# One wide score product per chunk and head for items 0 to 7 of a linear-attention kernel, and end tables turned ahead of item 0's own products

## The chip, the cores and the metric

The kernel runs on one NeuronCore of a Trainium2 chip. The metric is the device time of one execution in microseconds (us), measured from outside the program; a profile's span (first to last instruction) is a little shorter. All data is float32.

## The reference

Two layers follow each other. The first is a linear attention with a decaying state (B = 4 batches, H = 8 heads, S = 768 tokens, head size 48):

```python
for t in range(S):
    kt, vt, rt = (k[:, :, t], v[:, :, t], r[:, :, t])
    cur = np.einsum('bhd,bhe->bhde', u[None] * kt, vt)
    y[:, :, t] = np.einsum('bhd,bhde->bhe', rt, state + cur)
    state = w[None, :, :, None] * state + np.einsum('bhd,bhe->bhde', kt, vt)
```

The second sends each token (the 384 values of its 8 heads) to one of 8 experts, `max(x @ w1[e], 0) @ w2[e]`, scaled by a softmax gate; a sigmoid decides whether a token takes its own best expert or that of its predecessor. The change touches the first layer alone.

## The kernel before, in words

**Work items.** The attention is cut into 16 items: one batch and one pair of heads each (`n = b * HP + hp`, HP = 4). The two heads of a pair lie on partitions 0 to 47 and 64 to 111. The 768 tokens are 6 chunks of 128. For one item, TensorE (PE) does these stages:

- `scores` (L284 to 299): for each chunk the products of all its keys with all its queries, into one of two PSUM pairs of banks, three chunks each (`g` = 0 and 1). VectorE (DVE) multiplies each group by a mask, `kept`, into the SBUF tile `am` (L299), so that only earlier keys count.
- `own` (L267): the product of each token with its own key, times `vT` on DVE (L282), into the output bank `y`.
- `added` (L250): what each chunk adds to the state, into PSUM `T`, and `states` (L260): the running state over chunks, a scan on DVE.
- `inside` (L301): `am` times the values, added to `y`. `before` (L310): the state ahead of each chunk times the decayed queries `rw`, added to `y`. ScalarE (ACT) then copies `y` to `xT` (L327).
- `turn` (L332): transposes of the output, two ACT copies, and for the last pair of a batch a DMA to DRAM. `logits` (L345): the router's products, once per batch.

**Around them.** GpSimd (POOL) makes three tiles per item in `scale` (L205): `rw` (queries times powers of the decay), `ke` (keys times powers of the decay, from the table `endT`), `pd` (queries times keys). DVE makes `kw`, the keys divided by the powers (L246); for items 0 to 2 it makes `rw` too. `endT` holds each head's end powers with tokens on partitions: `ends` copies them out of the power table on ACT (L168, L169), `turn_ends` (L171) transposes them on PE and copies the result on ACT (L176).

**The order.** `run` (L362) writes the order of every engine's instructions out by hand, so each engine's queue holds what the code says in that order. In the step of item n the code issues, among others, `inside(n-1)`, `before(n-1)`, `scores(n+1)` (from n = 5 on; `scores(n)` before that), `own(n)`. In the step of item 0 it is `scores(0)`, `own(0)`, `turn_ends` for the three other head pairs, `warm(3)` (three transposes of the identity), `added(0)`. `banks` (L186) hands out the two PSUM pairs in turn, one per call. Loads of an item (`rk`, `kv`, `vT`) are issued on SyncE's queue three items ahead. After item 15 the experts follow, in one stream without a barrier.

**The score products of before.** A chunk's 128 keys are taken as two halves of 64 (L291 to 298). The first half meets all 128 queries, the second only the last 64, since earlier queries do not see later keys (item 0 takes all 128 for both). Each product is 48 rows by 64 columns of PE's array, and so uses one quarter of it: the row half follows from the head, the column half from `f = c % 2 ^ o`. In odd chunks the two halves change places, so that the long product falls on either column half in turn; the host stores the tokens of `k` and `v` of odd chunks with their halves swapped (`_tokens`, L1764), and `kept` has a second mask for them (L1693 to 1696). There are 24 such products per item. A float32 product is two matmul instructions in the trace, each with its weight load.

The parts that the change touches:

Of the kernel before, what the change touches and what calls it, by code (L numbers as in the profile page):

```python
# [20 lines left out]
P = 128  # L21
B, H, S, DH = 4, 8, 768, 48
HP = H // 2
DP = 64
# [25 lines left out]
W_LO, W_HI = 0.8, 1.25  # L50
C2 = NCH // 2
AHEAD = 4
VB = NCH * 2 * DH
LATE = (B * HP - 2, B * HP - 1)

# [7 lines left out]
class Attention:  # L63
# [127 lines left out]
    def load(self, n):  # L191
        nc = self.nc
        b, hp = divmod(n, HP)
        rk, vT, kv = self.rks[n % AHEAD], self.vTs[n % AHEAD], self.kvs[n % (AHEAD + 1)]
        if n:
            nc.sync.dma_start(out=rk.rearrange("p a c t -> p (a c t)"), in_=self.rk_d[b, hp])
        else:
            for z in (slice(0, C2), slice(C2, NCH)):
                nc.sync.dma_start(out=rk[:, :, z], in_=self.rk_d[b, hp].rearrange("p (a c t) -> p a c t", a=2, c=NCH)[:, :, z])
        nc.sync.dma_start(out=kv, in_=self.kv_d[b, hp])  # L200
        nc.sync.dma_start(out=vT.rearrange("p a c t -> p (a c t)"), in_=self.vT_d[b, hp])
        self.items[n].update(b=b, hp=hp, rT=rk[:, 0], kT=rk[:, 1], vT=vT,
                             k=kv[:, :VB].rearrange("p (c x) -> p c x", c=NCH), v=kv[:, VB:])

    def scale(self, n, ahead=None):  # L205

        nc, t = self.nc, self.items[n]
        t["ke"] = self.two.tile([P, NCH, 2 * DH], F32, name="ke")
        t["pd"] = self.two.tile([P, NCH, P], F32, name="pd")
        t["rw"] = self.four.tile([P, NCH, P], F32, name="rw")  # L210
        hp = t["hp"]

        def ke(p):
            z = slice(p, NCH if n == 0 else NCH - 1, 2)
            nc.gpsimd.tensor_mul(t["ke"][:, z], t["k"][:, z], spread(self.endT[:, p, hp], 1, len(range(NCH)[z])))  # L215

        def pd(i):
            z = slice(i * C2, (i + 1) * C2)
            nc.gpsimd.tensor_mul(t["pd"][:, z], t["rT"][:, z], t["kT"][:, z])  # L219
# [64 lines left out]
    def scores(self, n, g):  # L284

        nc, t = self.nc, self.items[n]
        if g == 0:
            t["am"] = self.two.tile([P, 2, 2, 3, P], F32, name="am")
        sc = self.banks("sc")[:, :, :3 * P].rearrange("p h (c t) -> p h c t", t=P)
        for i in range(3):  # L290
            c = 3 * g + i  # L291
            for o in range(2):
                for h in range(2):
                    q, f = slice(h * DP, h * DP + DH), c % 2 ^ o

                    x = o * DP if n else 0
                    nc.tensor.matmul(sc[f * DP:(f + 1) * DP, h, i, x:], lhsT=t["kw"][q, c, o * DP:(o + 1) * DP],  # L297
                                     rhs=t["rw"][q, c, x:], start=True, stop=True)
        return lambda: nc.vector.tensor_mul(t["am"][:, g], sc, spread(self.kept[:, g:g + 3], 1, 2))  # L299

    def inside(self, n):  # L301
        nc, t = self.nc, self.items[n]
# [59 lines left out]
    def run(self, router, fetch, heads):  # L362
# [162 lines left out]
def general_attention(tc, rk_d, kv_d, wu, wg_d, x_d, ident, lt):  # L525

    nc = tc.nc
    with tc.tile_pool(name="g1", bufs=1) as g1, tc.tile_pool(name="g2", bufs=2) as g2, \
         tc.tile_pool(name="gy", bufs=1, space=PSUM) as gy, \
         tc.tile_pool(name="gps", bufs=2, space=PSUM) as gps:  # L530
        ones = g1.tile([P, 2], F32, name="g_ones")
        nc.vector.memset(ones, 0.0)
        for i in range(2):
            nc.vector.memset(ones[i * DP:(i + 1) * DP, i:i + 1], 1.0)
        turned = g1.tile([P, P], F32, name="g_turned")
        nc.vector.tensor_copy(turned[:, :DP], ident[:, DP:])
        nc.vector.tensor_copy(turned[:, DP:], ident[:, :DP])
        with tc.For_i(0, HP, 1) as hp:
            wu_t = g1.tile([P, 2], F32, name="g_wu")
            nc.sync.dma_start(out=wu_t, in_=wu[bass.ds(hp, 1)].rearrange("o p x -> (o p) x"))  # L540
            with tc.For_i(0, B, 1) as b:
                def of(ap):
                    return ap[bass.ds(b, 1), bass.ds(hp, 1)].rearrange("o q p x -> (o q p) x")

                r_t = g1.tile([P, S], F32, name="g_r")
                k_t = g1.tile([P, S], F32, name="g_k")
                v_t = g1.tile([P, NCH, 2, DH], F32, name="g_v")
                nc.sync.dma_start(out=r_t, in_=of(rk_d)[:, :S])
                nc.sync.dma_start(out=k_t, in_=of(rk_d)[:, S:])
                nc.sync.dma_start(out=v_t.rearrange("p c i e -> p (c i e)"),  # L550
                                  in_=of(kv_d)[:, 2 * NCH * DH:4 * NCH * DH])
                yp = gy.tile([P, 2, 512], F32, name="g_y")
                for e in range(DH):
                    vp = gps.tile([P, 2, 512], F32, name="g_vp")
                    for c in range(NCH):
                        for i in range(2):
                            nc.tensor.matmul(
                                vp[i * DP:(i + 1) * DP, c // 3, (c % 3) * P:(c % 3 + 1) * P],
                                lhsT=v_t[:, c, i, e:e + 1].to_broadcast([P, DP]),
                                rhs=turned if c % 2 else ident,  # L560
                                start=True, stop=True)
                    kv = g2.tile([P, S], F32, name="g_kv")
                    nc.vector.tensor_mul(kv.rearrange("p (g t) -> p g t", g=2),
                                         k_t.rearrange("p (g t) -> p g t", g=2), vp[:, :, :3 * P])
                    sv = g2.tile([P, S + 1], F32, name="g_sv")
                    nc.vector.memset(sv[:, 0:1], 0.0)
                    nc.vector.tensor_tensor_scan(sv[:, 1:], wu_t[:, 0:1].to_broadcast([P, S]), kv, 0.0,
                                                 Alu.mult, Alu.add)
                    z = g2.tile([P, S], F32, name="g_z")
                    nc.vector.scalar_tensor_tensor(z, kv, wu_t[:, 1:2], sv[:, :S], Alu.mult, Alu.add)  # L570
                    nc.vector.tensor_mul(z, z, r_t)
                    for c in range(NCH):
                        o = (c % 3) * 2 * DH + 2 * e
                        nc.tensor.matmul(yp[:, c // 3, o:o + 2], lhsT=z[:, c * P:(c + 1) * P], rhs=ones,
                                         start=True, stop=True)
                y = g1.tile([P, 2, 3, 2, DH], F32, name="g_ys")
                for g in range(2):
                    for i in range(2):
                        nc.vector.tensor_copy(
                            y[:, g, :, i, :],  # L580
                            yp[:, g, :6 * DH].rearrange("p (c e i) -> p c e i", c=3, i=2)[:, :, :, i])
                nc.sync.dma_start(
                    out=x_d.rearrange("(b c p) (h j) -> b h p c j", b=B, p=P, h=HP)
                    [bass.ds(b, 1), bass.ds(hp, 1)].rearrange("o q p c j -> (o q p) c j"),
                    in_=y.rearrange("p g c i e -> p (g c) (i e)"))
# [1178 lines left out]
def _tokens(a, np):  # L1764

    x = a.reshape(B, HP, 2, NCH, 2, DP, DH)
    x = np.stack([x[:, :, :, c, ::-1 if c % 2 else 1] for c in range(NCH)], 2)
    return x.transpose(0, 1, 4, 5, 2, 3, 6).reshape(B, HP, P, NCH * 2 * DH)


# [35 lines left out]
```

## Time and profile before

| | |
|---|---|
| time, three runs | 376.53, 377.59, 377.77 us (median 377.59) |
| the profiled execution | 378.4 us, of which the span is 376.7 us |
| TensorE clock granted, mean | 0.996 of full speed |
| PE busy | 361.5 us, 96% of the span |
| DVE, ACT, POOL busy | 244.8, 110.5, 152.3 us |
| attention | to about 107 us of the span, then the experts |

In the views below, a row of the timeline gives the start in us, the busy time in us, the engine, the line of the kernel, the operation, the tiles written and read, the shapes, and behind x the number of instructions merged in the row; in brackets stands how long the engine was idle before it and what ended the wait. PE is the matmul, PEld the weight load that belongs to it; "issue" means that the profile shows nothing that the engine waited for. The busy time of a row of matmuls includes the flight of the last one (some 0.2 to 0.3 us), so the length of a stage is read from its start to the start of the next.

### The profile page before, as it was taken

Reading aid. Unit: us, or ns where it says so; the run is one execution under the profiler, and the core shown is the slowest. Engines: PE = TensorE matmul, PEld = TensorE weight load, DVE = VectorE, ACT = ScalarE, POOL = GpSimd, SP = SyncE. Lnnn points to the kernel's source line nnn. Section 1 sums busy time; section 2 is a strip of 40 time slices with the busy share of each in tenths; the row PEclk is TensorE's granted clock in tenths of the full one; section 3 lists DMA queues with packets and bytes.
Section 4 is the critical chain, followed back from the end, with each engine's and each line's share of the span. In section 5 each row is a group of like instructions: output and inputs, shape, how many; then the busy total and the mean of one; then the engine's idle time right before and its main releaser. Section 6 shows DMA issues by size and latency. Waiting matters only on the chain. (4 is left out here: it accounts for less than half of the span.)

```text
span 376.7 us, 9667 instructions
## 1 busy us (share of the span) xinstructions
PE 361.5 (96%) x3844; PEld 318.7 (85%) x3844; DVE 244.8 (65%) x711; ACT 110.5 (29%) x304; POOL 152.3 (40%) x212
## 2 busy tenths in 40 slices
PE   7998899999999999999999999999999999999992
PEld 6766777777769998989899999999999998989971
DVE  6887778788834835886557666857767767555300
ACT  4222232223523212322332233333243233331210
POOL 8789999789512055212333113313233023021012
PEclk9999999999999999999999999999999999999998
DMA  7999998992568748713352452264165065072011
GB/s 256 411 407 408 404 409 314 338 357 106 196 194 298 269 169 336 260 35 127 121 198 62 155 216 78 56 218 186 36 209 220 14 220 202 19 259 114 2 41 37
DMA packets 17764, 74.93 MB, mean 199 GB/s; under 512 B 2778, under 2 KB 6624, under 8 KB 15408
## 3 DMA queue, kind: packets, MB, share of 16 engines
q1 hardware_dynamic: 10336, 56.89, 40.7%
q0 software_dynamic: 3424, 9.48, 7.3%
q10 hardware_dynamic: 3952, 7.87, 5.6%
q8 instruction: 32, 0.52, 0.6%
q14 instruction: 20, 0.16, 0.1%
HBM read 64.79 MB, written 9.47 MB: 197 GB/s over the span
## 5 line engine op out<-in xcount | busy, mean ns | idle before, releaser
L1358 POOL DMA_INDIRECT out_dram<-yo,sid x27 | 26.6, 985 | 115.8 <-ACT yo L1353 92.3
L1209 PE MATMUL h<-exT,w1t 128*128 128x168 f32 (+4 forms) x240 | 54.9, 327 | 0.0
L1213 DVE TENSOR_TENSOR hT<-h,hs 128x168 f32<-128x168 f32 (+3 forms) x60 | 21.1, 351 | 46.2 <-PE h L1209 29.6
L1132 POOL DMA_INDIRECT xg<-x_d,gid x29 | 31.2, 1076 | 30.3 <-DVE gid L899 19.2
L1209 PEld LDWEIGHTS h<-exT,w1t 128*128 128x128 f32 x240 | 41.6, 190 | 0.3 <-issue 0.3
L1159 PE MATMUL h<-exT,w1t 128*128 128x168 f32 (+2 forms) x192 | 37.3, 332 | 0.0
L299 DVE TENSOR_TENSOR am<-pair,kept 128x768 f32<-128x768 f32 x32 | 30.1, 953 | 11.0 <-PE pair L297 10.8
L1278 PE MATMUL y<-factors,sums 128*128 128x192 f32 x168 | 36.8, 326 | 0.0
L219 POOL TENSOR_TENSOR pd<-rk 128x384 f32<-128x384 f32 x32 | 31.8, 1014 | 8.9 <-PE y L276 6.3
L1209 PE MATMUL h<-xs,ws 128*128 128x168 f32 (+4 forms) x144 | 35.3, 327 | 0.0
L1159 PEld LDWEIGHTS h<-exT,w1t 128*128 128x128 f32 x192 | 30.9, 190 | 2.0 <-issue 0.2
L1278 PEld LDWEIGHTS y<-factors,sums 128*128 128x128 f32 x168 | 29.0, 190 | 0.2
L1209 PEld LDWEIGHTS h<-xs,ws 128*128 128x128 f32 x144 | 25.5, 190 | 4.3 <-ACT hs L1216 1.2
L297 PE MATMUL pair<-rw,kw 48*64 48x128 f32 (+1 forms) x768 | 23.4, 249 | 1.9 <-issue 1.7
L236 POOL TENSOR_TENSOR rw<-rk,tab 128x384 f32<-128x384 f32 x26 | 23.6, 930 | 0.4 <-DMA rk<-in_rk_dram 0.4
L306 PE MATMUL y<-am,kv 128*64 128x128 f32 x360 | 22.9, 276 | 0.3
L1278 PE MATMUL y<-w2t,hT 128*128 128x192 f32 x96 | 23.0, 328 | 0.0
L297 PEld LDWEIGHTS pair<-rw,kw 48*64 48x64 f32 x768 | 19.9, 133 | 3.4 <-issue 2.4
L1146 DVE COPY exT<-tp 128x384 f32<-128x384 f32 (+5 forms) x29 | 13.8, 485 | 13.2 <-PE tp L1145 13.1
L215 POOL TENSOR_TENSOR ke<-kv,endT 128x288 f32<-128x288 f32 (+1 forms) x32 | 21.8, 704 | 0.9 <-DMA kv<-in_kv_dram 0.9
L306 PEld LDWEIGHTS y<-am,kv 128*64 128x64 f32 x360 | 19.4, 137 | 2.2 <-issue 1.1
L327 ACT COPY xT<-y 128x768 f32<-128x768 f32 x15 | 12.0, 801 | 29.0 <-PE y L319 29.0
(304 smaller groups left out, 735.4 us busy)
## 6 DMA issues: line engine op xcount, KB each, us to landing
w1t<-in_w_dram SPq DMA_DIRECT2D x8, 1536.0 KB, 6.9
w2t<-in_w_dram SPq DMA_DIRECT2D x8, 1536.0 KB, 7.4
rk<-in_rk_dram SPq DMA_DIRECT2D x15, 768.0 KB, 10.3
kv<-in_kv_dram SPq DMA_DIRECT2D x16, 584.0 KB, 8.5
vT<-in_vT_dram SPq DMA_DIRECT2D x16, 384.0 KB, 6.3
x_d<-x ACTq DMA_DIRECT2D x4, 1152.0 KB
w1t<-in_w_dram SPq DMA_DIRECT2D x2, 768.0 KB
w2t<-in_w_dram SPq DMA_DIRECT2D x2, 768.0 KB, 5.2
```

Source lines behind the costliest of these rows:

```text
L215: nc.gpsimd.tensor_mul(t["ke"][:, z], t["k"][:, z], spread(self.endT[:, p, hp], 1, len(range(NCH)[z])))
L219: nc.gpsimd.tensor_mul(t["pd"][:, z], t["rT"][:, z], t["kT"][:, z])
L236: engine.tensor_mul(t["rw"][:, z], t["rT"][:, z], spread(pw, 1, z.stop - z.start))
L297: nc.tensor.matmul(sc[f * DP:(f + 1) * DP, h, i, x:], lhsT=t["kw"][q, c, o * DP:(o + 1) * DP], rhs=t["rw"][q, c, x:], start=True, stop=True)
L299: return lambda: nc.vector.tensor_mul(t["am"][:, g], sc, spread(self.kept[:, g:g + 3], 1, 2))
L306: nc.tensor.matmul(t["y"][h][p * DP:(p + 1) * DP, c2 * P:(c2 + 1) * P], lhsT=t["v"][:, (2 * c + h) * DH:(2 * c + h) * DH + DP], rhs=t["am" ...
L1132: self.nc.gpsimd.indirect_dma_start(out=xg[:n], out_offset=None, in_=self.x_d[:rows], in_offset=bass.IndirectOffsetOnAxis(ap=u["gid"][:n, ...
L1159: nc.tensor.matmul(h[:, :n], lhsT=u["w1"][:, m, kk, :], rhs=u["xT"][:, kk, :], start=(kk == 0), stop=(kk == DK - 1))
L1209: nc.tensor.matmul(out, lhsT=a, rhs=b, start=start and k == 0, stop=stop and k == len(terms) - 1, skip_group_check=True)
L1213: nc.vector.tensor_tensor(out, a, b, op=Alu.add)
L1278: return lambda: nc.tensor.matmul(bank[:, x * half:(x + 1) * half], lhsT=a, rhs=b, start=(j == 0 and x == 0), stop=(j == FK // 2 - 1), ski ...
L1358: self.nc.gpsimd.indirect_dma_start(out=out.rearrange("n (h d) -> (n h) d", h=2) if half else out, out_offset=bass.IndirectOffsetOnAxis(ap ...
```

## The change

A constant `WIDE = 2` makes the items of batches 0 and 1, items 0 to 7, wide. For them a chunk's product per head is one product of 128 keys and 128 queries (48 rows by 128 columns, half of the array), 12 per item in place of 24. Their tokens lie in natural order in `k` and `v`, so `ke` takes the table of even chunks for all chunks and the mask is `kept[:, 0]` for all chunks. Items 8 to 15 are as before. In the step of item 0, `turn_ends(1..3)` is issued ahead of `own(0)`, and `warm(3)` is gone.

```diff
+WIDE = 2
...
-            nc.gpsimd.tensor_mul(t["ke"][:, z], t["k"][:, z], spread(self.endT[:, p, hp], 1, len(range(NCH)[z])))
+            nc.gpsimd.tensor_mul(t["ke"][:, z], t["k"][:, z], spread(self.endT[:, 0 if t["wide"] else p, hp], 1, len(range(NCH)[z])))
...
         for i in range(3):
             c = 3 * g + i
+            if t["wide"]:
+                for h in range(2):
+                    q = slice(h * DP, h * DP + DH)
+                    nc.tensor.matmul(sc[:, h, i], lhsT=t["kw"][q, c], rhs=t["rw"][q, c], start=True, stop=True)
+                continue
             for o in range(2):
                 for h in range(2):
                     q, f = slice(h * DP, h * DP + DH), c % 2 ^ o
 
-                    x = o * DP if n else 0
+                    x = o * DP
                     nc.tensor.matmul(sc[f * DP:(f + 1) * DP, h, i, x:], lhsT=t["kw"][q, c, o * DP:(o + 1) * DP],
                                      rhs=t["rw"][q, c, x:], start=True, stop=True)
-        return lambda: nc.vector.tensor_mul(t["am"][:, g], sc, spread(self.kept[:, g:g + 3], 1, 2))
+        kept = spread(self.kept[:, 0], 1, 3) if t["wide"] else self.kept[:, g:g + 3]
+        return lambda: nc.vector.tensor_mul(t["am"][:, g], sc, spread(kept, 1, 2))
...
                 self.reciprocals(1)
+                self.turn_ends(slice(1, HP))
                 self.own(0)
-                self.turn_ends(slice(1, HP))
-                self.warm(3)
                 self.added(0)
```

The host's `_tokens` swaps the halves of odd chunks for batches 2 and 3 only. `general_attention`, a path that runs only for decays out of range, gets a loop for each of the two layouts; it doesn't run on this input, and its code lies behind the end of the stream.

The order of PE's instructions changes in two places (`order` rows: line, operation, tile written and tiles read, stationary columns by moving columns, count; one row entry is one product, two instructions on the chip). In the step of item 0, before, from its scores (L297, into `pair`) to its `inside` (L306); L276 is `own`, L175 `turn_ends`, L165 `warm`, L258 `added`:

```order
L297 MATMUL pair_149<-rw,kw 64x128 x12
L297 MATMUL pair_148<-rw,kw 64x128 x12
L276 MATMUL y<-pd,w_t 64x384 x4
L175 MATMUL pair_149<-ident,end 128x128 x6
L165 MATMUL pair_148<-ident 128x128 x3
L258 MATMUL mp<-kv_162,ke 64x48 x10
L306 MATMUL y<-am,kv_162 64x128 x12
```

The same place now; lines are shifted by the edit (L296 is the wide product, L176 `turn_ends`, L277 `own`, L259 `added`, L313 `inside`):

```order
L296 MATMUL pair_149<-rw,kw 128x128 x6
L296 MATMUL pair_148<-rw,kw 128x128 x6
L176 MATMUL pair_149<-ident,end 128x128 x6
L277 MATMUL y<-pd,w_t 64x384 x4
L259 MATMUL mp<-kv_162,ke 64x48 x10
L313 MATMUL y<-am,kv_162 64x128 x12
```

The six transposes moved ahead of `own`, into the bank pair that the first group of scores used, and the three of `warm` are gone. In the step of item 5, before, PE's rows from `inside` of item 4 (L306) over `before` of item 4 (L319) into the first group of scores of item 6:

```order
L306 MATMUL y<-am,kv_166 64x128 x12
L319 MATMUL y<-rw,S 48x128 x10
L297 MATMUL pair_149<-rw,kw 64x128 x2
L297 MATMUL pair_149<-rw,kw 64x64 x2
L297 MATMUL pair_149<-rw,kw 64x128 x2
L297 MATMUL pair_149<-rw,kw 64x64 x2
L297 MATMUL pair_149<-rw,kw 64x128 x2
L297 MATMUL pair_149<-rw,kw 64x64 x2
```

The same place now, with both groups of scores and `own` (L277):

```order
L313 MATMUL y<-am,kv_166 64x128 x12
L326 MATMUL y<-rw,S 48x128 x10
L296 MATMUL pair_148<-rw,kw 128x128 x6
L296 MATMUL pair_149<-rw,kw 128x128 x6
L277 MATMUL y<-pd,w_t 64x384 x4
```

Nothing moved here: 24 products became 12, with twice the stationary columns. One call of `banks` less makes the two PSUM pairs change places from here on. The rows of DVE, ACT, POOL and SyncE are the same as before up to line numbers, outside of the code that doesn't run.

More of the change, by code (lines that the diff above doesn't have):

```diff
@@ L540, in general_attention @@
             nc.sync.dma_start(out=wu_t, in_=wu[bass.ds(hp, 1)].rearrange("o p x -> (o p) x"))
[L541 to L555, printed above, removed]
-                        for i in range(2):
[L557 to L585, printed above, removed]
@@ new lines, in general_attention, with of @@
+            for first, last in ((0, WIDE), (WIDE, B)):
+                with tc.For_i(first, last, 1) as b:
+                    def of(ap):
+                        return ap[bass.ds(b, 1), bass.ds(hp, 1)].rearrange("o q p x -> (o q p) x")
+                    r_t = g1.tile([P, S], F32, name="g_r")
+                    k_t = g1.tile([P, S], F32, name="g_k")
+                    v_t = g1.tile([P, NCH, 2, DH], F32, name="g_v")
+                    nc.sync.dma_start(out=r_t, in_=of(rk_d)[:, :S])
+                    nc.sync.dma_start(out=k_t, in_=of(rk_d)[:, S:])
+                    nc.sync.dma_start(out=v_t.rearrange("p c i e -> p (c i e)"),
+                                      in_=of(kv_d)[:, 2 * NCH * DH:4 * NCH * DH])
+                    yp = gy.tile([P, 2, 512], F32, name="g_y")
+                    for e in range(DH):
+                        vp = gps.tile([P, 2, 512], F32, name="g_vp")
+                        for c in range(NCH):
+                            for i in range(2):
+                                nc.tensor.matmul(
+                                    vp[i * DP:(i + 1) * DP, c // 3, (c % 3) * P:(c % 3 + 1) * P],
+                                    lhsT=v_t[:, c, i, e:e + 1].to_broadcast([P, DP]),
+                                    rhs=turned if c % 2 and first else ident,
+                                    start=True, stop=True)
+                        kv = g2.tile([P, S], F32, name="g_kv")
+                        nc.vector.tensor_mul(kv.rearrange("p (g t) -> p g t", g=2),
+                                             k_t.rearrange("p (g t) -> p g t", g=2), vp[:, :, :3 * P])
+                        sv = g2.tile([P, S + 1], F32, name="g_sv")
+                        nc.vector.memset(sv[:, 0:1], 0.0)
+                        nc.vector.tensor_tensor_scan(sv[:, 1:], wu_t[:, 0:1].to_broadcast([P, S]), kv, 0.0,
+                                                     Alu.mult, Alu.add)
+                        z = g2.tile([P, S], F32, name="g_z")
+                        nc.vector.scalar_tensor_tensor(z, kv, wu_t[:, 1:2], sv[:, :S], Alu.mult, Alu.add)
+                        nc.vector.tensor_mul(z, z, r_t)
+                        for c in range(NCH):
+                            o = (c % 3) * 2 * DH + 2 * e
+                            nc.tensor.matmul(yp[:, c // 3, o:o + 2], lhsT=z[:, c * P:(c + 1) * P], rhs=ones,
+                                             start=True, stop=True)
+                    y = g1.tile([P, 2, 3, 2, DH], F32, name="g_ys")
+                    for g in range(2):
+                        for i in range(2):
+                            nc.vector.tensor_copy(
+                                y[:, g, :, i, :],
+                                yp[:, g, :6 * DH].rearrange("p (c e i) -> p c e i", c=3, i=2)[:, :, :, i])
+                    nc.sync.dma_start(
+                        out=x_d.rearrange("(b c p) (h j) -> b h p c j", b=B, p=P, h=HP)
+                        [bass.ds(b, 1), bass.ds(hp, 1)].rearrange("o q p c j -> (o q p) c j"),
+                        in_=y.rearrange("p g c i e -> p (g c) (i e)"))
```

4 lines of the change are left out of this document (2 added, 2 removed).

## The prediction

> **What bounds the kernel now.** I read the page first, then the DMA view of the stage that changes, then the timeline of weight loads for breaks in PE's stream, then stage lengths on PE and the neighbours that would be late next. On the page, engine rows are busy us, share, instructions; the queue row is packets, MB, share:
>
> ```profile
> span 376.7 us, 9667 instructions
> PE 361.5 (96%) x3844; PEld 318.7 (85%) x3844; DVE 244.8 (65%) x711; ACT 110.5 (29%) x304; POOL 152.3 (40%) x212
> ...
> q8 instruction: 32, 0.52, 0.6%
> ```
>
> PE is the bound: all but 15 us of the span. So a change counts by what it does to PE's stream. The last row is a queue that carries instructions: 32 packets, 0.52 MB, 16 KB each. PE runs 2 x 3844 instructions, 7688, or 240 per packet; with its separate waits that is close to 256 of 64 bytes. So I read it as the supply of PE's program. The same view between 20 and 58 us:
>
> ```profile
> DMA  9999999999999999999999999999999999999998
> ...
> DMA packets 4234, 15.45 MB, mean 406 GB/s; under 512 B 402, under 2 KB 1170, under 8 KB 4225
> ...
> q8 instruction: 6, 0.10, 1.0%
> ```
>
> While items 2 to 8 run, the DMA engines are full with the items' loads, and only six packets of program come: one per 6.3 us. Now the weight loads on PE, where "issue" marks waits for which the profile has no releaser. The last groups are one stretch in full:
>
> ```profile
> 20.64 0.54 PEld L297 LDWEIGHTS pair<-rw,kw 48*64 48x64 f32 x23 [0.17 <-issue]
> ...
> 26.77 0.54 PEld L297 LDWEIGHTS pair<-rw,kw 48*64 48x64 f32 x23 [0.44 <-issue]
> ...
> 33.43 0.54 PEld L297 LDWEIGHTS pair<-rw,kw 48*64 48x64 f32 x22 [1.09 <-issue]
> ...
> 39.77 0.30 PEld L258 LDWEIGHTS mp<-kv,ke 128*48 128x48 f32 x9 [1.47 <-issue]
> ...
> 51.93 0.48 PEld L258 LDWEIGHTS mp<-kv,ke 128*48 128x48 f32 x17 [0.52 <-issue]
> 52.29 1.33 PEld L306 LDWEIGHTS y<-am,kv 128*64 128x64 f32 x24
> 53.79 0.58 PEld L319 LDWEIGHTS y<-rw,S 48*48 48x48 f32 x18 [0.17 <-issue]
> 54.21 0.14 PEld L297 LDWEIGHTS pair<-rw,kw 48*64 48x64 f32 x2
> 54.31 0.16 PEld L319 LDWEIGHTS y<-rw,S 48*48 48x48 f32 x2
> 54.32 1.14 PEld L297 LDWEIGHTS pair<-rw,kw 48*64 48x64 f32 x46
> 55.59 0.21 PEld L276 LDWEIGHTS y<-pd,w_t 48*64 48x64 f32 x8
> 56.40 0.59 PEld L338 LDWEIGHTS pair<-ident,xT 112*128 112x128 f32 x6 [0.60 <-DVE am L299]
> 57.12 0.17 PEld L258 LDWEIGHTS mp<-kv,ke 128*48 128x48 f32 x4
> 57.53 0.44 PEld L258 LDWEIGHTS mp<-kv,ke 128*48 128x48 f32 x16 [0.24 <-issue]
> ```
>
> The waits in the middle of a stage (after 24 or 25 of 48, 11 of 20, 3 of 20, 4 of 20) are the point. From 51.93 to 57.53 there are 17 + 24 + 18 + 2 + 2 + 46 + 8 + 6 + 4 = 127 loads, with as many matmuls 254, with the stage waits 256: one packet. The others stand at that distance or twice it. So PE stops where one packet of program ends and the next has not come. These stops add to 0.17 + 0.44 + 1.09 + 1.47 + 0.52 + 0.24 = 3.93 us. Item by item PE needs 254 or so of 256 per item: the program is used as fast as the full DMA engines bring it.
>
> **The change part by part.**
>
> *Fewer instructions.* A wide item has 12 products fewer, 24 matmuls and 24 loads: some 210 instructions in place of 258. From L319 at 47.91 (quoted below) to L319 at 53.79 an item takes 5.88 us, of which 0.52 is a stop: 5.36; with the 0.48 us that is added below 5.84 us. A packet then lasts 256 / 210 x 5.84 = 7.1 us, longer than the 6.1 to 6.7 us between stops today (20.64, 26.77, 33.43, 39.77). So I take all stops up to item 7 as gone: -3.9 us. The packet that serves items 8 and 9 meets the old density, 258 per item or 5.4 us, while the loads, which follow PE by buffer releases, still fill the DMA engines: up to some 0.9 us (6.3 less 5.4) may come back there, once or twice, or nothing. I take +0.4 (0 to 1.5).
>
> *Longer streams.* Two rows from item 0 give the price of a pass, and the rest gives stages from start to start:
>
> ```profile
> 6.33 1.30 PEld L297 LDWEIGHTS pair<-rw,kw 48*64 48x64 f32 x48 [0.17 <-ACT endT L176]
> ...
> 9.68 0.64 PEld L175 LDWEIGHTS pair<-ident,end 128*128 128x128 f32 x6 [0.60 <-issue]
> ```
>
> ```profile
> 36.78 1.24 PE L297 MATMUL pair<-rw,kw 48*64 48x128 f32 x48
> 37.95 0.47 PE L258 MATMUL mp<-kv,ke 128*48 128x48 f32 x11
> ...
> 46.45 1.53 PE L306 MATMUL y<-am,kv 128*64 128x128 f32 x24
> 47.91 0.79 PE L319 MATMUL y<-rw,S 48*48 48x128 f32 x18
> ...
> 49.72 0.87 PE L276 MATMUL y<-pd,w_t 48*64 48x384 f32 x8
> ...
> 106.47 0.90 PE L319 MATMUL pair<-rw,S 48*48 48x128 f32 x20
> 107.30 1.49 PE L350 MATMUL y<-xT,wp 128*32 128x384 f32 x12
> ```
>
> Six full-array passes of 128 columns take 0.64 us, 107 ns each; the 48 quarter-array ones of item 0 take 1.30 us, four in 108 ns: quarters run side by side. From item 1 on the second products stream only 64 columns, which saves a quarter of that. A wide product fills a row half, so two can run at once. No row here has two row halves at full width; the nearest is `inside` (L306), 24 matmuls of 128 columns on column halves, two at once: 1.46 us to the next stage. Item 0, which has full products already, is unchanged. Its neighbour stages decide the rest: today L319, L297 and L276 all use quarters and follow without a seam, 47.91 to 49.72 or 1.81 us from L319 to L276. L319 followed by a stage with another split of the array takes 106.47 to 107.30, 0.83 us. So now 0.83 + 1.46 = 2.29, +0.48 us per item; for item 5, whose scores lie between two L258 stages, 1.46 against 1.17, +0.29. Items 6 and 7 pay in full (0.96). In items 1 to 4 PE waits in the second group of scores or at `own` for DVE and ACT, here item 2:
>
> ```profile
> 20.33 0.13 PEld L297 LDWEIGHTS pair<-rw,kw 48*64 48x64 f32 x1 [0.45 <-ACT xT L327]
> ```
>
> so a longer first group is partly free; I take half, 4 x 0.25 = 1.0. Sum +2.3 us (1.3 if items 1 to 4 hide it all, 3.2 if none).
>
> *Item 0.*
>
> ```profile
> 7.38 1.82 DVE L299 TENSOR_TENSOR am<-pair,kept 128x768 f32<-128x768 f32 x2 [0.52 <-PE pair L297]
> ...
> 8.79 1.55 POOL L215 TENSOR_TENSOR ke<-kv,endT 128x288 f32<-128x288 f32 x2
> 8.88 0.88 PE L276 MATMUL y<-pd,w_t 48*64 48x384 f32 x8 [1.01 <-POOL pd L219]
> ...
> 9.82 0.97 DVE L282 TENSOR_TENSOR y<-y,vT 128x768 f32<-128x768 f32 x1
> ...
> 10.81 0.79 PE L258 MATMUL mp<-kv,ke 128*64 128x48 f32 x20
> ...
> 11.43 1.50 PE L306 MATMUL y<-am,kv 128*64 128x128 f32 x24
> ```
>
> PE idles 1.01 us ahead of `own`, then does transposes and `warm` from 9.68 to 10.81. The transposes now wait for their bank, which DVE's first mask step leaves at about 8.3, and run to 9.05; `own` starts at 9.1 in place of 8.88, behind it the DVE step of L282 ends at 11.0; `added` waits for `ke`, ready at 10.34. `inside` starts at 11.0 in place of 11.43: -0.4 us (-0.2 if DVE's `kw` and `rw` of item 1 eat half). `endT` comes earlier, and nobody reads it before item 1's `ke`. No DMA and no other queue is passed.
>
> *At nothing:* the mask step reads a repeated mask in the same shape (L299's 0.91 us in a pair), `ke` another column of the same table; DVE and POOL have slack there. The general path is not run.
>
> *What is late next.* POOL is busy without a gap from item 4 on:
>
> ```profile
> 29.71 1.98 POOL L219 TENSOR_TENSOR pd<-rk 128x384 f32<-128x384 f32 x2
> 31.64 1.69 POOL L236 TENSOR_TENSOR rw<-rk,tab 128x384 f32<-128x384 f32 x2
> ...
> 33.94 0.90 PE L276 MATMUL y<-pd,w_t 48*64 48x384 f32 x7
> ```
>
> `pd` of item 4 is done at 31.69 and PE uses it at 33.9: 2.2 us of room, and by then PE gains about 1. Item 5's `rw` is done at 33.33 and used at 36.78. So POOL doesn't bind for a gain of this size.
>
> **Sum.** -3.9 + 0.4 + 2.3 - 0.4 = -1.6 us. The profiled execution took 378.4 us, 0.8 above the median 377.59 of the three runs; I apply the difference to the median: 376.0.
>
> **The rivals.**
> - *The stops are not a matter of count.* If PE stops for something tied to time, or the supply isn't what the rows say, the 3.9 us stay and the wide products cost 2.3 less 0.4: 379.5. For it: no row names the releaser. Against: the even distance of 256. The Trainium skill, "Runtime: NRT & Kernel Launch", section "Instruction fetch mechanics", says that blocks of 16 KiB, 256 instructions, are streamed ahead and that crossing into the next is mostly hidden; by that the change would come out slower in this way. The trace agrees with its block of 256, and differs on "hidden": up to 1.47 us at one crossing. Chance 0.08.
> - *Row halves one after another.* If two full-width halves don't overlap, their matmuls or loads, each round doubles: 24 x 0.107 = 2.6 us against 1.31, +1.3 on top for each of eight items, and PE, not the supply, sets the pace: about 384 (377.6 + 2.3 + 8 x 1.3 - 4.3 = 386 at most, less what DVE and ACT waits hide). It decides from rounds over some 0.15 us. For it: no row has this shape. Against: quarters overlap across row halves today. The Trainium skill, "TensorEngine Tiling (Array Packing)", section "Tiling Modes", lists 64x128 as two independent tiles; no run so far shows it. Chance 0.05.
> - *The stops come back behind item 8.* The shifted packet ends fall on the dense items 8 to 10 with DMA full, and again later where loads fill the DMA engines; 1.2 us are given back: 377.2. Chance 0.11.
> - *The experts' start doesn't move*, since its first gather or weight piece comes when it did: 377.6. Against: the gather is set off by steps that follow the attention, which ends earlier. Chance 0.04.
>
> **How the numbers follow.** The forecast has 0.72. Its own range: cost 1.3 to 3.2 and 0 to 1.5 given back, not all together, 374.6 to 377.1. The third and fourth rival reach 377.6; I put the range at 374.6 to 377.8, leaving out the two slow rivals (0.13) and a little at the fast end. A measurement of this kernel can tell some 0.3%, 1.1 us, from no change. Of the forecast's 0.72, four fifths lie beyond that: faster 0.59. Same: 0.13 + 0.11 + 0.04 = 0.28. Slower: 0.08 + 0.05 = 0.13.
>
> **What would show it.** Right: the waits on "issue" inside stages up to about 55 us are gone or under 0.3 us together, wide scores take 1.4 to 1.5 us to the next stage, L319 to `own` 2.2 to 2.3, `inside` of item 0 starts near 11.0, and `own` of item 7 (its loads at 55.59 today) starts 1.2 to 2.2 us earlier. Wrong: wide scores of 2.6 us; stops of an us at other places in items 1 to 7; or POOL or a load named as releaser of PE there.

## The result, and the profile after

| | before | after |
|---|---|---|
| time, median of 13 executions each | 377.59 us (376.17 to 380.15) | 380.37 us (377.91 to 382.63) |
| ratio | 1 | 1.0066 (95%: 1.0043 to 1.0090) |
| profiled execution | 378.4 us, span 376.7 | 377.91 us, span 376.1 |

The kernel after is slower by 0.7%, where 1.6 us less were forecast. A second comparison gave 379.80 against 377.79 us, a ratio of 1.0048 (1.0024 to 1.0073). Ratios leave out the few executions of a slower state and are not the quotients of the medians. The profiled execution of after is the fastest of its 13, and that of before is one of its slower ones: on these two traces alone the change would look like a gain of 0.5 us. So the readings below use four traces of after (of executions of 377.91, 379.67, 381.91 and 380.14 us) and two of before (378.4 and 377.72).

The page of after: 195 matmuls and as many weight loads fewer, one packet of program fewer, and 3 us more PE time (PE 361.5 before).

```profile
span 376.1 us, 9276 instructions
...
PE 364.5 (97%) x3649; PEld 320.9 (85%) x3649; DVE 245.2 (65%) x711; ACT 110.5 (29%) x304; POOL 152.4 (41%) x212
...
q8 instruction: 31, 0.51, 0.6%
```

The stretch from 20 to 58 us, where the stops were: busy time of each engine, then granted clock, DMA share and GB/s. First before, then after:

```profile
20.00:58.00 38.00, 34.54 (x782) 26.28 (x779) 28.71 (x55) 10.10 (x27) 34.79 (x45) 1.00 1.02 406
```

```profile
20.00:58.00 38.00, 37.93 (x679) 29.36 (x675) 29.71 (x56) 10.29 (x27) 36.02 (x48) 1.00 1.02 408
```

PE was busy for 34.54 of 38 us and is now for 37.93, with the DMA engines just as full: the stops there are gone. Behind item 8 they are back. PE's weight loads in after (L303 is the narrow product, L326 `before`):

```profile
53.24 1.13 PEld L303 LDWEIGHTS pair<-rw,kw 48*64 48x64 f32 x46
54.51 0.21 PEld L277 LDWEIGHTS y<-pd,w_t 48*64 48x64 f32 x8
...
70.55 0.35 PEld L326 LDWEIGHTS y<-rw,S 48*48 48x48 f32 x9 [0.17 <-issue]
71.94 0.36 PEld L326 LDWEIGHTS y<-rw,S 48*48 48x48 f32 x9 [1.04 <-issue]
...
77.31 0.26 PEld L326 LDWEIGHTS y<-rw,S 48*48 48x48 f32 x7
78.54 0.47 PEld L326 LDWEIGHTS y<-rw,S 48*48 48x48 f32 x13 [0.97 <-issue]
```

Item 7's `own` starts at 54.51 in place of 55.59, 1.1 us earlier where 1.2 to 2.2 had been named as the sign. Then two waits on "issue" in the middle of `before`, 1.04 and 0.97 us, give it back; before had one such wait there, of 0.65 us at 80.39. The stages that changed, in the rows of PE's matmuls (a stage's length is from its start to the next start):

```profile
36.21 1.61 PE L296 MATMUL pair<-rw,kw 48*128 48x128 f32 x24
37.75 0.65 PE L259 MATMUL mp<-kv,ke 128*48 128x48 f32 x20
...
46.86 0.90 PE L326 MATMUL y<-rw,S 48*48 48x128 f32 x20
47.69 1.61 PE L296 MATMUL pair<-rw,kw 48*128 48x128 f32 x24
49.23 0.88 PE L277 MATMUL y<-pd,w_t 48*64 48x384 f32 x8
```

A wide stage takes 1.54 us, L326 0.83 us, the two 2.37 us where 2.29 were forecast and 1.81 stood before. So two row halves do run side by side: the 24 matmuls of a stage start in pairs, 0.11 us from pair to pair.

**All traces by the same parts.** The trace has the start and landing of each packet of the instruction queue, and so each stop can be counted at its packet end (from start to start, which is 0.1 us more than the brackets; 0.1 us is the least that is counted). The attention is then cut as follows: start of item 0's scores; from there to item 0's `inside`; from there to the last batch's logits (L350, at 107.30 in before), less the stops and less half of the time at half clock ("attention bare"); from the logits to the end.

| trace | scores 0 | to inside 0 | stops to 58 / behind | at half clock | attention bare | rest |
|---|---|---|---|---|---|---|
| before, first | 6.33 | 5.10 | 4.51 / 0.92 | 0 | 90.44 | 269.39 |
| before, second | 7.73 | 4.33 | 3.58 / 0.63 | 0 | 90.57 | 269.09 |
| after, first | 6.31 | 4.93 | 0.10 / 2.33 | 0 | 93.76 | 268.72 |
| after, second | 7.03 | 4.93 | 0.10 / 3.20 | 0 | 93.72 | 269.00 |
| after, third | 7.22 | 4.93 | 0.10 / 2.45 | 6.83 | 93.23 | 268.86 |
| after, fourth | 6.74 | 4.93 | 0.10 / 3.96 | 0 | 93.81 | 268.90 |

The first column differs from execution to execution in both kernels and says nothing of the change. The others give the balance: bare attention +3.2 us, stops 3.9 less up to 58 us and 2.2 more behind, and one thing that the prediction does not have: in the third trace TensorE ran at half speed for 6.83 us.

### The profile page after: what moved, and what is told of

It is laid out like the page before. It is cut to its first block, busy times and chain, and to the rows that moved or that the text cites. A ratio compares the mean times of both kernels' runs of the same rounds, so it can differ in the third digit from the quotient of the medians.

```text
span 376.1 us, 9276 instructions
## 1 busy us (share of the span) xinstructions
PE 364.5 (97%) x3649; PEld 320.9 (85%) x3649; DVE 245.2 (65%) x711; ACT 110.5 (29%) x304; POOL 152.4 (41%) x212
## 5 line engine op out<-in xcount | busy, mean ns | idle before, releaser
L306 DVE TENSOR_TENSOR am<-pair,kept 128x768 f32<-128x768 f32 x32 | 29.9, 954 | 10.2 <-PE pair L296 5.5
L313 PE MATMUL y<-am,kv 128*64 128x128 f32 x360 | 22.9, 277 | 0.0
L313 PEld LDWEIGHTS y<-am,kv 128*64 128x64 f32 x360 | 19.4, 137 | 1.8 <-issue 1.1
L1271 DVE TENSOR_TENSOR factors<-w2t 128x192 f32<-128x192 f32 x56 | 19.7, 352 | 0.0
L1216 PE MATMUL h<-xs,w1t 128*128 128x168 f32 (+4 forms) x96 | 19.7, 328 | 0.0
```

The lines of the kernel that those rows point to most:

```text
L313: nc.tensor.matmul(t["y"][h][p * DP:(p + 1) * DP, c2 * P:(c2 + 1) * P], lhsT=t["v"][:, (2 * c + h) * DH:(2 * c + h) * DH + DP], rhs=t["am" ...
L1216: nc.tensor.matmul(out, lhsT=a, rhs=b, start=start and k == 0, stop=stop and k == len(terms) - 1, skip_group_check=True)
L1271: nc.vector.tensor_tensor(t[:, x], a, b, op=Alu.subtract)
```

## The experiments

**Traces again.** The two kernels unchanged.

> The kernel after, unchanged, for a second trace of it: the first trace is of an execution of 377.9 us, 2.5 us under the median 380.4 of the kernel. Theory A (program supply): the executions differ by PE's stops at the ends of 16 KB packets. Then a trace near 380.4 us has the same stage lengths (wide scores 1.54 us, L326 0.83 us) and 4 to 5 us of stops in place of 2.2 us, most of them behind item 8, where packets meet some 255 instructions per item again. Theory B (the wide product itself or its neighbours vary): the stops stay near 2.2 us and the 2.5 us lie in longer wide scores or in waits for DVE, ACT or POOL in items 1 to 7.

Measured: 379.80 us median; its trace is of 379.67 us. The stage lengths are those of the first trace, and the stops sum to 3.30 in place of 2.43 us; of the 1.8 us between the two spans 0.9 are stops and 0.7 a later start of item 0. Theory A holds in kind, though its 4 to 5 us of stops were too many, and B falls: wide stages and waits are unchanged.

> The kernel before, unchanged, for a second trace of it. Theory A (program supply): the stages have the lengths of the first trace, and the stops between 16 and 108 us sum to 4 to 5.5 us again, most of them up to 58 us; the granted clock has no drop before the end. If the sum were 3 us or less, the first trace of before would be no typical one, and part of the loss of the kernel after would lie there.

Measured: 377.72 us, stops of 4.21 us, no drop of the clock. The first trace of before was typical in that.

> The kernel after, unchanged, for a third trace of it. Its executions range from 378 to 382.6 us, and a good third of them have a granted clock of 0.992 or less, so a trace may fall on one of these. Theory A: such a trace shows the clock at 0.5 for one or two stretches of 3.4 us, right behind a stretch in which PE stood still for over 1 us, and is 1.5 to 3.5 us longer for it; without a drop the time is 378 to 380.5 and the stops behind item 8 are 2 to 3.5 us.

> The kernel after, unchanged, for a fourth trace of it: as for the third.

Measured: 381.91 and 380.14 us. The fourth has 4.06 us of stops, above the 2 to 3.5 expected, and no lowered clock before the program's end. The third has one long stop, and the clock falls behind it. Its weight loads:

```profile
71.76 0.35 PEld L326 LDWEIGHTS y<-rw,S 48*48 48x48 f32 x9 [0.17 <-issue]
73.98 0.35 PEld L326 LDWEIGHTS y<-rw,S 48*48 48x48 f32 x9 [1.88 <-issue]
74.18 0.14 PEld L303 LDWEIGHTS pair<-rw,kw 48*64 48x64 f32 x2
74.20 0.25 PEld L326 LDWEIGHTS y<-rw,S 48*48 48x48 f32 x2
74.29 1.70 PEld L303 LDWEIGHTS pair<-rw,kw 48*64 48x64 f32 x46
```

and its stretches (the number ahead of the last two is the granted clock):

```profile
71.34:74.75 3.41, 1.66 (x49) 1.36 (x48) 2.40 (x5) 0.05 (x1) 3.18 (x4) 1.00 1.04 393
74.75:78.16 3.41, 3.41 (x63) 2.23 (x57) 1.35 (x2) 0.75 (x1) 0.34 (x1) 0.50 0.78 316
78.16:81.58 3.42, 3.42 (x36) 3.05 (x33) 3.16 (x5) 0.70 (x2) 3.42 (x5) 0.50 0.52 167
81.58:85.00 3.42, 3.42 (x91) 2.78 (x87) 1.24 (x6) 1.18 (x3) 1.15 (x2) 1.00 0.93 340
```

In the stretch from 71.34 PE is busy for 1.66 of 3.41 us; the next two run at 0.50, with dense scores taking 1.70 us (the row at 74.29) in place of 1.13 (53.24 in the first trace). The time without use is paid once as a stop of 2.0 us and once more as 3.4 us of lost clock.

**The parts alone.**

wide_alone is after with the step of item 0 as before; order_alone is before with the step of item 0 as after, the same edit the other way round.

```diff
-                self.turn_ends(slice(1, HP))
                 self.own(0)
+                self.turn_ends(slice(1, HP))
+                self.warm(3)
```

> The wide products for items 0 to 7 with the step of item 0 ordered as before (own, turn_ends, warm, added). Theory A: the stops up to 58 us are gone as in the kernel after, the packet ends lie some 12 instructions off those of the kernel after, and the time is that of after plus the 0.2 us that the prologue gained: 379.5 to 381. Theory C (the reordered prologue is what costs, through the phase of everything behind it): the time is at or below 377.6.

> The kernel before with the prologue of after alone. Theory A: inside of item 0 starts 0.2 to 0.4 us earlier, the stops up to 58 us stay at 3 to 4 us, and the time is 376.8 to 377.8. Theory C: the time rises by 2 us or more.

Measured: wide_alone 379.91 us, ratio 1.0022 (0.9986 to 1.0058); order_alone 378.11 us, ratio 1.0010 (0.9991 to 1.0029). Theory C falls: its 2 us for the order alone lie outside order_alone's interval. Neither part alone is clear of no change, and wide_alone's executions spread from 376.79 to 382.92 us, so these ratios do not settle how the loss divides between the two; the traces have to. The trace of wide_alone has stops of 0.35 us up to 58 us and 2.35 behind, and again 6.83 us at half clock behind one of 1.12 us; that of order_alone has 3.41 us at half clock behind a wait of 2.6 us in the experts' part. What the order does shows in item 0, where the 0.2 to 0.4 us of gain that A expected did not come. Before, second trace:

```profile
8.78 1.82 DVE L299 TENSOR_TENSOR am<-pair,kept 128x768 f32<-128x768 f32 x2 [1.93 <-PE pair L297]
8.98 0.26 PEld L276 LDWEIGHTS y<-pd,w_t 48*64 48x64 f32 x8
9.86 0.64 PEld L175 LDWEIGHTS pair<-ident,end 128*128 128x128 f32 x6 [0.61 <-issue]
...
11.06 0.95 DVE L282 TENSOR_TENSOR y<-y,vT 128x768 f32<-128x768 f32 x1
...
12.06 1.18 PEld L306 LDWEIGHTS y<-am,kv 128*64 128x64 f32 x22
```

and after, second trace:

```profile
8.11 1.82 DVE L306 TENSOR_TENSOR am<-pair,kept 128x768 f32<-128x768 f32 x2 [0.96 <-PE pair L296]
...
9.21 0.85 PE L176 MATMUL pair<-ident,end 128*128 128x128 f32 x6 [0.58 <-DVE am L306]
...
9.99 0.21 PEld L277 LDWEIGHTS y<-pd,w_t 48*64 48x64 f32 x8 [0.17 <-issue]
...
10.93 0.97 DVE L283 TENSOR_TENSOR y<-y,vT 128x768 f32<-128x768 f32 x1 [0.46 <-PE y L277]
...
11.95 1.29 PEld L313 LDWEIGHTS y<-am,kv 128*64 128x64 f32 x24 [0.50 <-DVE y L283]
```

Before, `own` runs right behind the scores, its product is there when DVE is through with the masks, and `inside` starts 12.06 - 8.78 = 3.28 us after the mask step. After, `own` stands behind the transposes (L176), which wait for that mask step; DVE then waits 0.46 us for `own`, PE 0.50 us for DVE, and it is 3.84 us. The first trace of before is the odd one: its scores started early, at 6.33, and `own` had to wait for POOL's `pd`. Of seven traces with the old order and narrow scores in item 0 (these experiments' included) five take 4.33 to 4.37 us from scores to `inside`, two, with scores at 6.35 or earlier, 4.86 and 5.10; with the new order it is 4.90 to 4.93 in all. So the order gives 0.2 us back at best and costs 0.6 us as a rule.

**More items wide.** The constant `WIDE` at 3 (items 0 to 11) and at 4 (all).

> All 16 items wide. Theory A: some 210 instructions per item throughout, so the two stops behind item 8 (1.18 and 1.02 us in the trace of after) are gone too, while items 8 to 15 pay 0.37 + 0.2 us each, 8 x 0.57 = 4.6 us: 380.4 + 4.6 less 2 to 4 us of stops, 381 to 383. Theory B (no stops to save behind item 8 in the typical execution): 380.4 + 4.6 = 385.

> Items 0 to 11 wide. Theory A: the packets behind item 8 now hold 210 instructions per item, so the two stops near 72 and 79 us go (2.2 to 2.5 us), four more items pay 0.4 to 0.57 each (1.6 to 2.3 us), and items 12 to 15 are dense where the DMA engines have idle times: few stops come back. Time 379 to 380.5, and a spread of the executions as small as with all items wide (under 1.5 us without clock drops). Rival (the density step itself, wherever it lies, brings stops and a drop of the clock): two stops of an us move to 95 to 107 us and the time is 381.5 or more.

Measured: all_wide 380.67 us (380.26 to 381.16), ratio 1.0074 (1.0045 to 1.0103), stops of 0.39 us in all. PE behind item 8:

```profile
58.00:108.00 50.00, 50.00 (x846) 38.10 (x846) 39.13 (x69) 16.12 (x41) 37.80 (x45) 1.00 0.70 241
```

Eight more wide items leave the time where it was within 1 us: bare attention rises to 98.00, by 4.3 us, while 2.7 us of stops go and, by the estimate further down, 0.7 us of lost clock; none of the six executions shows a lowered clock and they lie within 0.9 us. That is theory A, a little better than it said (381 to 383). three_wide: 381.12 us (379.11 to 382.41), ratio 1.0056 (1.0025 to 1.0086), stops of 0.39 us. A is right on the stops, and wrong on the time and the spread: five of the twelve executions have a lowered clock. The one trace taken shows a drop with its wait; what came ahead of the others is not known. PE's loads and DVE's rows, then the stretches:

```profile
94.09 0.21 PEld L277 LDWEIGHTS y<-pd,w_t 48*64 48x64 f32 x8
96.66 0.83 PEld L345 LDWEIGHTS pair<-ident,xT 112*128 112x128 f32 x6 [2.36 <-DVE am L306]
```

```profile
91.80 3.87 DVE L837 TENSOR_SCALAR si<-si 128x12 int32<-128x12 int32 x1
95.59 0.16 DVE L838 TENSOR_SCALAR si<-si 128x12 int32<-128x12 int32 x1
```

```profile
93.51:96.92 3.41, 1.72 (x43) 0.91 (x34) 3.41 (x4) 1.71 (x6) 2.13 (x3) 1.00 0.58 206
96.92:100.34 3.42, 3.42 (x44) 3.14 (x44) 2.91 (x5) 2.49 (x8) 2.33 (x3) 0.50 0.01 2
```

A wait of another kind, for DVE, is followed by the same half clock.

**Lighter loads.** Items 5 to 15 load no `kv` and items 4 to 15 no `vT`, in both kernels; what is computed in them, and the routing, is not the reference's, and the limits on tokens per expert are lifted.

```diff
-        nc.sync.dma_start(out=kv, in_=self.kv_d[b, hp])
-        nc.sync.dma_start(out=vT.rearrange("p a c t -> p (a c t)"), in_=self.vT_d[b, hp])
+        if n <= AHEAD:
+            nc.sync.dma_start(out=kv, in_=self.kv_d[b, hp])
+        if n < AHEAD:
+            nc.sync.dma_start(out=vT.rearrange("p a c t -> p (a c t)"), in_=self.vT_d[b, hp])
```

> The kernel before with fewer loads: items 5 to 15 load no kv and items 4 to 15 no vT (they compute with those of earlier items), and the limits on tokens per expert are lifted, since the routing changes. Theory A (a packet of program waits behind the item loads): with the DMA engines mostly idle from some 25 us on, a packet starts about 1 us after PE passes a packet's end, and the stops after 25 us fall from some 4.5 us to under 0.8 us; the time falls by 3 to 4.5 us, to 373 to 375. Rival S (the stops go with PE's own instructions, whatever the DMA engines do): the stops stay, and the time stays within 0.5 us.

> The same cut of loads in the kernel after. Theory A: its stops behind item 8 go too, no execution shows a lowered clock, and what is left between before_light and after_light is the wide product's own price, 3 us (8 items of some 0.4) less 0.2 for the prologue: after_light is slower by 2.5 to 3.5 us, 376 to 378. Rival S: the stops of after stay, and the two differ by 2 us as the full kernels do.

Measured: before_light 375.42 us, ratio 0.9939 (0.9903 to 0.9975); after_light 377.34, ratio 0.9977 (0.9946 to 1.0007). The DMA view of before_light from 40 to 66 us (busy tenths):

```profile
DMA  9739999999940789930009489200477941009727
...
DMA packets 1505, 5.17 MB, mean 199 GB/s; under 512 B 96, under 2 KB 864, under 8 KB 1499
...
q8 instruction: 5, 0.08, 1.2%
```

In before the same stretch moved 9.69 MB at 373 GB/s. From 40 us on before_light has no stop over 0.05 us, with PE's program unchanged: S falls. Up to 40 us the loads still catch up and 2.2 us of stops stay, so the gain is 2.4 us and not 3 to 4.5. after_light has no stop over 0.1 us and no lowered clock, and still takes 1.9 us more; its bare attention is 94.29 against 91.71. That is the price of the wide products by itself, 2.6 us. Against the 2.2 us of stops that before_light keeps this gives less than the 1.9 us measured: the spans of the two traces differ by 0.7 us only. The trace of after_light is of its fastest execution, 1.3 us under the median, and where the others spend that was not traced.

**What one packet does.** From the traces (us):

| kernel | PE passes a packet's end | next packet starts, lands | PE at the next end | goes on | stop |
|---|---|---|---|---|---|
| before | 26.77 | 30.73, 31.94 | 32.21 | 33.43 | 1.22 |
| before | 33.43 | 37.24, 38.27 | 38.21 | 39.77 | 1.56 |
| after, wide item | 39.55 | 41.75, 42.84 | 46.86 | 46.87 | 0 |
| after, dense item | 65.47 | 69.54, 70.47 | 70.76 | 71.94 | 1.18 |
| after, third trace | 66.69 | 71.74, 72.67 | 71.97 | 73.98 | 2.02 |
| before_light | 55.83 | 56.42, 57.37 | 60.95 | 60.95 | 0 |

Of 46 stops over 0.25 us in 14 traces, 43 end 1.2 to 1.6 us after their packet has landed. So a stop is the packet's lag (mostly 2 to 5 us where the loads fill the DMA engines, 0.6 in before_light at 55.83), plus 1.0 us to land and some 1.4 us to use, less PE's time for the packet before: some 5.3 us where items are dense (4.8 to 6.7), 6.6 to 8.1 where they are wide.

**Can the supply be relieved for less?** In mid_wide, made from before, only items 2 to 5 are wide (`wide=n in WIDE`, with `WIDE = (2, 3, 4, 5)`). In long_own the narrow items 2 to 7 issue `own` three times:

```diff
-        for p in range(2):
+        for p in list(range(2)) * (3 if 1 < n < 8 else 1):
```

> Only items 2 to 5 wide, with the prologue of before (the general path, which does not run here, keeps the layout of before). Theory A (a stop is the time from passing a packet's end to the next packet's use, some 6.3 us while the loads fill the DMA engines, less the PE time of that packet): the stops up to 40 us (3.3 us in both traces of before) go, the four items pay 3 x 0.5 + 0.37 = 1.9 us, and items 6 to 10 have two or three stops of 0.5 to 1 us. Attention ends 0.5 us earlier to 0.5 us later than in before: 377 to 378.5, and no gain worth keeping. Rival W (the wide product's price is what hurts, the stops hardly matter): 377.8 + 1.9 = 379.7 or more.

> The kernel before, with the products of own issued three times over in items 2 to 7 (they overwrite the same values, so the output is the same): 16 more instructions and 1.28 us more PE time per item, 6 x 1.28 = 7.7 us in all. Theory A: a packet then lasts 256 / 274 x 6.56 = 6.1 us in place of 5.2, so the stops between 25 and 58 us fall from some 4 us to under 1 us, and the time rises by 3.5 to 5 us only. Rival S (the stops do not depend on how long PE takes for a packet): they stay, and the time rises by 7 us or more.

Measured: mid_wide 378.61 us, ratio 1.0009 (0.9988 to 1.0030). Up to 40 us 0.2 us of stops are left, and the dense items behind have new ones:

```profile
42.76 0.32 PEld L303 LDWEIGHTS pair<-rw,kw 48*64 48x64 f32 x14 [0.82 <-issue]
...
49.03 0.30 PEld L303 LDWEIGHTS pair<-rw,kw 48*64 48x64 f32 x11 [1.08 <-issue]
...
55.35 0.26 PEld L303 LDWEIGHTS pair<-rw,kw 48*64 48x64 f32 x10 [1.13 <-issue]
```

The sum of all stops is 4.69 us, as in before: they moved. long_own took 387.09 us (four executions), ratio 1.0209 (1.0160 to 1.0258), against 381.5 to 383 by A, and so within what rival S gave (7 us or more): its bare attention rose by 8.0 us (98.47) and the stops did not fall but moved, from 4.1 to 1.9 us up to 58 us and from 0.8 to 5.1 behind. The packets there started 4.1 to 5.0 us late, so that even 5.8 us of PE time per packet was too short. A's 6.3 us was no constant, and its sum fell with it. This run does not tell A from S; that stops depend on the loads, and not on PE's program alone, rests on before_light, and that they depend on PE's time per packet on the wide items of after and mid_wide.

**Does PE's standing lower the clock?** One mask step of DVE, of the first scores of item 10, is issued three times in hold_2, and five times in hold_4.

```diff
-                self.scores(ahead, 0)()
+                masked = self.scores(ahead, 0)
+                for i in range(3 if n == 9 else 1):
+                    masked()
```

> The kernel before with one mask step of DVE (first group of scores of item 10, near 68 us) issued three times; it writes the same values again, takes 0.9 us each time, and PE has to wait for its bank: PE stands some 1 to 1.5 us once, without any stop of the program supply. Theory K (PE standing in a stretch of 3.4 us is what lowers the clock): the wait costs 1 to 1.5 us, and a lowered clock (0.992 or less) shows in more executions than the 9 of 75 of the kernel before, perhaps in a third. Rival Q (a lowered clock has nothing to do with PE standing): its share stays near one in eight.

> The same with five issues in place of one, so that PE stands 2.5 to 3.3 us once. Theory K: most executions show a lowered clock of one or two stretches of 3.4 us at 0.5, which costs 1.5 to 3.4 us on top of the wait: time 381.5 to 384.5, and the stretch at 0.5 begins within 3.4 us of the wait in the trace. Rival Q: the time rises by the wait alone, to 380.3 to 381, with the clock as in before.

Measured: hold_2 380.91 us, ratio 1.0060 (1.0026 to 1.0093); hold_4 383.28 us, ratio 1.0136 (1.0083 to 1.0189). The waits were longer than expected, 2.38 us in hold_2 and 4.37 in hold_4. The loads and stretches of hold_4:

```profile
68.28 0.21 PEld L276 LDWEIGHTS y<-pd,w_t 48*64 48x64 f32 x8
72.86 1.03 PEld L338 LDWEIGHTS pair<-ident,xT 112*128 112x128 f32 x6 [4.37 <-DVE am L299]
```

```profile
67.42:70.83 3.41, 1.73 (x52) 0.93 (x42) 2.87 (x3) 0.80 (x1) 1.50 (x2) 1.00 1.03 394
70.83:74.24 3.41, 1.38 (x8) 1.11 (x10) 3.35 (x4) 0.00 (x0) 2.36 (x3) 0.50 0.28 107
74.24:77.66 3.42, 3.42 (x44) 3.16 (x44) 2.98 (x6) 0.70 (x2) 1.34 (x2) 0.50 0.82 293
```

The trace of hold_2 has its wait and no drop behind it:

```profile
70.42 0.58 PEld L338 LDWEIGHTS pair<-ident,xT 112*128 112x128 f32 x6 [2.38 <-DVE am L299]
```

```profile
68.00:72.00 4.00, 2.28 (x42) 1.47 (x40) 3.93 (x5) 0.70 (x2) 3.12 (x4) 1.00 1.03 391
72.00:76.00 4.00, 4.00 (x112) 3.10 (x110) 3.60 (x8) 0.80 (x1) 2.17 (x4) 1.00 0.96 322
```

It also has a second wait for DVE, of 2.34 us at 96.79, which the edit did not ask for, and again no drop. The mean clock is 0.994 to 0.997 in the traces that have a drop at the program's end alone, where PE is done, and 0.984 to 0.992 in those with an earlier one. Counting 0.992 or less as an earlier drop and 0.993 as none, 13 of 92 executions of before have one, 6 of 12 of hold_2, 6 of 6 of hold_4, and 11 of 25 of after. The share grows with the wait, and in hold_4 the drop stands right behind it, so a long wait of PE does bring a drop (theory K); one of 2.4 us does not do so each time.

## Why the prediction was wrong, point by point

- **Stops up to 58 us, -3.9.** Right: 4.51 and 3.58 us before, 0.10 in each trace of after (the brackets of the prediction leave out 0.1 us per stop). The rival that the stops are no matter of count is refuted by this and by before_light. The rule of the Trainium skill ("Runtime: NRT & Kernel Launch", "Instruction fetch mechanics"), that the crossing of a block is mostly hidden, gave the right sign for another reason; the traces show crossings of up to 2.0 us.
- **"I take +0.4 (0 to 1.5)" for what comes back.** This step failed: it is 2.2 us (2.33 to 3.96 us behind 58 us, 0.63 and 0.92 before). The step took 6.3 us of supply less 5.4 us of item. But the packets behind item 8 that stop PE take 5.7 to 7.4 us from a packet's end to the use of the next, and one to four of them in a trace meet dense items while the loads last, up to some 86 us, and cost 0.3 to 2.0 us each. Before, the items there are as dense, but two packets in each trace started only 0.9 to 2.3 us after the end was passed, though the DMA engines were nearly as full (from 56 to 62 us a share of 0.95 and 0.98 in the two traces of before, 0.98 to 0.99 in the first two of after); why they came so soon is open. The rival of stops behind item 8 was right in kind and had 1.2.
- **"Longer streams", +2.3.** The stage was read well (2.37 against 2.29 us). What failed is "a longer first group is partly free; I take half": 3.2 us were paid, the upper bound. The waits of items 1 to 4 that were to hide it stood in part for stops: less the stops, L319 to L276 took 1.9, 2.3, 1.9 and 1.6 us in items 1 to 4 of before, and takes 2.4, 2.7, 2.4 and 2.4 after. Only item 2, the one whose row was shown, had a wait in this place to hide some of it.
- **Item 0, -0.4.** Failed: -0.2 in the trace that it was read from, +0.6 in most others.
- **Not in the sum: the clock.** 11 of 25 executions against 13 of 92, at 1.7 us for one stretch of 3.41 us at half speed and 3.4 for two: by estimate worth some 0.7 us in the mean.

With the middle of each, -3.9 + 2.2 + 3.2 + 0.4 (item 0) + 0.7 = +2.6 us; the medians differ by 2.8 and 2.0. Of the 4.2 us between this and the -1.6 that were forecast, 1.8 lie in what comes back, 0.9 in the longer streams, 0.8 in item 0 and 0.7 in the clock. Row halves one after another did not occur (12 rounds start within 1.34 us, 0.11 us apart). The experts' part is some 0.3 us shorter, so nothing was lost there. POOL and the loads did not bind, as forecast: from item 1 to 60 us PE waited for POOL 0.6 us in all, before as after.

## What to carry to other kernels

In this kernel a stall of a supply was not removed by thinning out one stretch: ask where the supply is short next, with the same lag and the density that follows, and charge the stops that return there. Here a wait of PE of 2 us cost more than its length where the clock fell behind it, so count the share of executions with a lowered clock, not only the median. And take a price that rests on one place of one trace from a second trace as well: both the -0.4 of item 0 and the half that "was free" came from the state of a single execution.

## What the runs showed of the hardware that was not expected

- PE's clock can fall to half for one or two stretches of 3.41 us behind a wait. In three of the traces above PE was busy for about half of the stretch ahead of the drop (1.66, 1.72 and 1.73 of 3.41 us). But in wide_alone it was busy for 2.56, with a stop of 1.1 us, and in hold_2 a stretch with 1.70 had no drop behind it (counted back in steps of 3.413 us from the drop at its end); stops of 1.2 to 1.6 us in before brought none in its two traces. So neither the length of one wait nor the busy share of one stretch settles it; what else does is open. The Trainium skill, "TensorE: Matmul & The Clock Gate", "Part 1: The HAM clock gate", gives free-running windows of 3413 ns, and half and full speed as an idle and a busy state, which the trace agrees with (stretches of 3.41 us, clocks of 0.50 and 1.00); its warning is of idle gaps of over some 3.4 us, and here a stop of 2.0 us had a drop behind it.
- The lag of a packet of program behind full DMA engines is no constant: for the ends passed between 20 and 40 us it was 2.2 to 2.8 us in the first trace of after and 3.7 to 4.0 us in that of before, at 408 and 406 GB/s from 20 to 58 us. Why it differs is open.
- A DVE step on 128x12 elements took 3.87 us in three_wide (L837 above) and 3.85 us in hold_2, where it stands ahead of the second wait, but 0.82 us in the first trace of after. In both POOL was busy without a gap meanwhile, and one of its steps ended within 0.1 us of DVE's. That POOL held DVE up is only argued; it wasn't tried.
